# Retention, mixture of experts and rational network on one core: counts of groups of six in the natural blocks' banks, and a product bank for the conversions beside the first expert

## The chip, the cores and the metric

The kernel runs on one core of one Trainium2 chip. The metric is the device time of one launch in microseconds (us), median of several runs. Engines: PE (TensorE, matrix products), DVE (VectorE), ACT (ScalarE), POOL (GpSimd), SP (SyncE, which issues DMAs). Matrix products land in PSUM, eight banks of 512 four-byte words in each of 128 partitions; DVE and ACT empty them.

## What is computed

```python
for t in range(S):                                   # _attn_ref: 4 x 8 heads, 768 steps, 64 wide
    state = gamma * state + outer(k[t], v[t])
    y[t] = scale * q[t] @ state
# x = y as (3072, 512)
logits = x @ w_gate                                  # _moe_ref: 8 experts, 384 tokens each
for idx in np.argsort(-logits.flatten()):            # greedy: best logit first, while the expert has room
    ...
out[mask] = np.maximum(x[mask] @ w1[e], 0) @ w2[e]
h = out @ w_in                                       # _moe2_ref
g = P(h) / (Q(h) + 1e-6)                             # P cubic, Q quadratic in |h|
return g @ w_out
```

## The kernel before, in words

**Stage one** (0 to about 170 us) takes the 24 blocks of 128 tokens in turn (`for j in range(NCH)`). For a block PE does, in an order written out by hand: `trans` (two transposes, L352), `scores` (L382), `state` (L395), `natural` of the block before (L424: back to token-major, with the eight logits beside it) and `yout` (L407, L411). The transposes and the natural blocks share three PSUM banks, the pool `pt` (`NPT = 3`): `trans` takes two, `natural` two (one emptied by ACT, L428; one by DVE, L426). `scores`, `state`, `yout` and the conversions have banks of their own.

Beside this, two jobs run in stage one. *Conversions:* the weights `w_in` and `w_out` come as 64-bit numbers; `conv` (L239) makes float32 words of a 128x512 block with three DVE operations, L241, L243 and L244, and one on ACT, L242. Its intermediate words `t1` lie in a PSUM tile `cvp` in stage one. *Counts:* for the routing, `first(c0, c1)` (L448) makes one-hot choices and 128 threshold comparisons for a group of blocks (six DVE operations, L438 to L454), and `first_count` (L457) lets PE count them (L460) into a bank of its own from `pt`, and adds the result to `cn0` (L462). Groups are of three blocks, and the counts follow three blocks after.

**Stage two** starts with the routing of the first expert. Then the experts run one after another. For each, `mm1` (w1, L814) and `mm2` (w2) make the expert's output in eight steps; then sixteen steps of `mm3` (w_in, L814), `rat1` to `rat3` (the rational function: ACT L868 to L870, POOL L871, DVE L872, L873, L888 to L890), `gsplit`, and `mm4` (w_out, L910) three steps behind. `xt` (L798) transposes the next expert's tokens. `mm1`, `mm3` and `xt` share three PSUM banks, the tag `w` with `bufs=3`; the accumulators take four banks, the routing one. The bank of `mm3(i)` is free when L873 of step i has read it.

The routing of the next expert is a chain of small DVE operations and small PE products (L628, L641 and others), of which `chain.hop()` puts two links at a time into PE's order. PE waits at a link until DVE has done the link before.

Beside the first expert alone, twelve conversions are still to do: six blocks of `w_out` in the first eight steps (`job_conv`, tiles `xg`) and six of `w_in` in the sixteen (`in_conv_a`, tiles `w2r`). Here `conv` is called without `t1`, so that all its words lie in SBUF.

The orders of PE, ACT and POOL are those in which the code is written (`manual_schedule`; ACT's from stage two on). DVE's order is set by the scheduler, from its own estimates, with the chain given priority (`PRIO`).

Of the kernel before, what the change touches and what calls it, by code (L numbers as in the profile page):

```python
# [24 lines left out]
NCH = B * NC  # L25
# [27 lines left out]
CST = 2  # L53
CRAMP = 2
ET = mybir.EngineType
PROENG = {ET.PE, ET.Pool}
# [118 lines left out]
def moe_kernel(ctx, tc, q, k, v, w_gate, w1, w2, w_in, w_out, a, b, cf, ci, out):  # L175
# [74 lines left out]
    with ExitStack() as pst:  # L250
# [164 lines left out]

        def natural(j):

            if j < 0:
                return
            x = XN[j] = wk.tile([128, HP, 128 + E], F32, name="xn", bufs=3)  # L420
            for g in range(2):
                p = pp.tile([128, 2, 128 + E], F32, name="pt", bufs=NPT)
                for e in range(2):
                    nc.tensor.matmul(p[:, e, :], XT[j][:, 2 * g + e, :], IW[:, 2 * g + e, :], start=True, stop=True)  # L424
                if g:
                    nc.vector.tensor_copy(x[:, 2:4], p)  # L426
                else:
                    nc.scalar.activation(x[:, 0:2], p, AF.Copy)  # L428
            nc.vector.tensor_reduce(Sl[:, j, :], x[:, :, 128:].rearrange("p a e -> p e a"), axis=AX.X, op=OP.add)
            for r in range(2):  # L430
                nc.sync.dma_start(xd[j * 128:(j + 1) * 128, :].rearrange("(q r) (a f) -> r q a f", r=2, a=HP)[r],
                                  x[r * 64:r * 64 + 64, :, 0:128])
# [14 lines left out]

        CM0 = {}  # L448

        def first(c0, c1):  # L450
            onehot(c0, c1)
            w = c1 - c0
            cm = CM0[c0] = wk.tile([128, w, J0], BF16, name="cm")
            nc.vector.tensor_tensor(cm, m[:, c0:c1, None].to_broadcast([128, w, J0]),  # L454
                                    cit[:, 0:J0].bitcast(F32)[:, None, :].to_broadcast([128, w, J0]), op=OP.is_ge)

        def first_count(c0, c1):  # L457
            p = pp.tile([J0, E], F32, name="pt", bufs=NPT)
            for c in range(c0, c1):
                nc.tensor.matmul(p, CM0[c0][:, c - c0, :], oh[:, c, :], start=c == c0, stop=c == c1 - 1)  # L460
            if c0:
                nc.vector.tensor_tensor(cn0, p, cn0, op=OP.add)  # L462
            else:
                nc.vector.tensor_copy(cn0, p)

        load(0, "qk")
# [18 lines left out]
        for j in range(NCH):  # L485
# [12 lines left out]
            state(j)  # L498
            natural(j - 1)
            if j % 3 == 0 and j >= 3:  # L500
                first(j - 3, j)
                if j > 3:
                    first_count(j - 6, j - 3)
            if j == NCH - 1:
                first_count(NCH - 6, NCH - 3)
            yout(j)
# [3 lines left out]
        while db < da:  # L510
            conv_b(db)
            db += 1
        first(NCH - 3, NCH - 1)
        natural(NCH - 1)
        first_count(NCH - 3, NCH - 1)
        first(NCH - 1, NCH)
# [269 lines left out]
    def w2_split(n, f):  # L786
# [4 lines left out]
        w2_load(n, f + 2)  # L791

    def xt(n, t):
        if t == 0:
            XTS[n] = mp.tile([128, 2, KD, CAP], F32R, name="xT", bufs=1)
        p = ps.tile([128, KD, 128], F32, name="w", bufs=3)
        for d in range(KD):
# [20 lines left out]
    def mm1(n, f):  # L818
        p = ps.tile([128, CAP], F32, name="w", bufs=3)
        w, x = W1S[n, f], XTS[n]  # L820
# [30 lines left out]
    def mm3(n, i):  # L851
        p = US[n, i] = ps.tile([128, CAP], F32, name="w", bufs=3)
        y = YS[n]
# [92 lines left out]
    def job_conv(j):  # L946
        if j < NLATE:
            CA[j] = mp.tile([128, KD * 128], I32, name="xg", bufs=TB)
            conv(rawx[:, j % 3], CA[j], mp.tile([128, KD * 128], I32, name="xg", bufs=TB))
            job_load(j + 3)  # L950
# [15 lines left out]
    def in_conv_a(j):  # L966
        if j >= len(NORES):
            return
        CA[j] = mp.tile([128, KD * 128], I32, name="w2r")
        conv(RX[j], CA[j], mp.tile([128, KD * 128], I32, name="w2r"))  # L970
        in_load(j + 2)
# [139 lines left out]
```

## Time and profile before

| | |
|---|---|
| median of 3 runs | 1081.24 us (1080.59 to 1082.49) |
| the profiled execution's own time | 1081.6 us |
| its span, first to last instruction | 1079.7 us |
| PE busy, share of the span | 1010.1 us, 94% |
| DVE, ACT, POOL busy | 775.5, 698.5, 629.1 us |
| stage one ends (last `yout`) | about 169 us |
| first expert, first product to last | about 202 to 334 us |
| every later expert | about 106 us |

The span is 1.9 us shorter than that execution's time. Busy times overlap. A matmul's record is the time in which it is in the engine, so that neighbouring records overlap by some tens of ns.

### The profile page before, as it was taken

How to read it: one execution, taken by the hardware profiler on the slowest of the kernel's cores; microseconds unless marked ns; L12 is line 12 of the kernel's file. 1: busy time of each engine (PE TensorE's matmuls, PEld its weight loads, DVE VectorE, ACT ScalarE, POOL GpSimd, SP SyncE). 2: the span in 40 equal slices, each digit the busy share in tenths (PEclk: the TensorE clock that was granted, in tenths of full speed). 3: DMA queues.
4: the chain of work that ended last, by engine and by line, in shares of the span. 5: the costliest groups of instructions: out<-in, count | busy, mean ns of one | idle time of the engine just before them, and what ended most of it. 6: DMA issues, size and time to landing. Idle time of an engine off the chain costs nothing.

```text
span 1079.7 us, 18280 instructions
## 1 busy us (share of the span) xinstructions
PE 1010.1 (94%) x6278; PEld 922.2 (85%) x6278; DVE 775.5 (72%) x1862; ACT 698.5 (65%) x1365; POOL 629.1 (58%) x612
## 2 busy tenths in 40 slices
PE   6999885679889999999999999999999999999995
PEld 5888774678779989998999899999998999989984
DVE  4899887678994788478747874787578756751773
ACT  6889882346684488458745874587358736873883
POOL 5677662464686367635663666366736663666452
PEclk9999997699999999999999999999999999999998
DMA  9999862523333212321232124212422142223110
GB/s 191 244 250 252 226 162 89 151 93 96 100 127 118 88 50 79 117 88 59 69 121 86 59 69 127 79 59 70 137 69 68 60 137 70 88 65 110 50 59 29
DMA packets 142028, 115.01 MB, mean 107 GB/s; under 512 B 56560, under 2 KB 122352, under 8 KB 141936
## 3 DMA queue, kind: packets, MB, share of 16 engines
q1 hardware_dynamic: 131184, 76.10, 26.7%
q0 software_dynamic: 10752, 37.75, 10.5%
q8 instruction: 49, 0.80, 0.3%
q14 instruction: 43, 0.35, 0.1%
HBM read 98.10 MB, written 15.73 MB: 105 GB/s over the span
## 4 chain that ended last, share of the span: by engine, by line
PE 63%; DVE 7%; ACT 2%; issue 2%; POOL 1%; POOLq 0%; DVEq 0%
PE w L814 30%; PE acc L910 22%; PE acc L814 8%; PE pr L628 1%; PE w L798 1%; DVE hg L825 1%; DVE cm L592 1%; ACT hg L824 0%; DVE t L872 0%; DVE t L890 0%; POOL qq L871 0%; DVE yT L842 0%; DVE qq L888 0%; DVE acc L889 0%; DVE pr L583 0%
## 5 line engine op out<-in xcount | busy, mean ns | idle before, releaser
L910 PE MATMUL acc<-woh,hg 128*128 128x512 f32 x1152 | 290.2, 397 | 4.8 <-ACT hg L895 4.5
L910 PEld LDWEIGHTS acc<-woh,hg 128*128 128x128 f32 x1152 | 212.8, 188 | 49.7 <-ACT hg L895 7.0
L871 POOL TENSOR_TENSOR qq<-qq,z 128x384 f32<-128x384 f32 x127 | 129.4, 1019 | 165.2 <-ACT z L869 163.7
L814 PE MATMUL w<-yT,wih 128*128 128x384 f32 x960 | 179.6, 339 | 0.1
L896 POOL TENSOR_TENSOR hg<-t,hg 128x384 fp32r<-128x384 f32 x127 | 131.6, 1037 | 81.4 <-ACT hg L895 53.1
L814 PEld LDWEIGHTS w<-yT,wih 128*128 128x128 f32 x960 | 166.4, 188 | 3.8 <-DVE yT L842 0.7
L814 PE MATMUL w<-xT,w1s 128*128 128x384 f32 x768 | 149.7, 343 | 0.6 <-ACT xT L800 0.6
L814 PE MATMUL acc<-hg,w2s 128*128 128x384 f32 x768 | 146.2, 339 | 0.3 <-DVE hg L825 0.3
L814 PEld LDWEIGHTS w<-xT,w1s 128*128 128x128 f32 x768 | 135.4, 192 | 1.9 <-ACT xT L800 0.8
L814 PEld LDWEIGHTS acc<-hg,w2s 128*128 128x128 f32 x768 | 132.7, 188 | 1.1 <-DVE hg L825 0.6
L888 DVE SCALAR_TENSOR_TENSOR qq<-qq,acc 128x384 f32<-128x384 f32 x128 | 70.8, 553 | 60.4 <-ACT acc L883 33.3
L248 POOL TENSOR_TENSOR w1s<-w1r,w1s 128x512 fp32r<-128x512 f32 x64 | 83.2, 1300 | 49.2 <-ACT w1s L247 48.4
L814 PE MATMUL w<-yT,wis 128*128 128x384 f32 x576 | 110.0, 339 | 1.1 <-DVE t L873 1.1
L248 POOL TENSOR_TENSOR w2s<-w2r,w2s 128x512 fp32r<-128x512 f32 x64 | 83.2, 1301 | 43.7 <-ACT w2s L247 43.4
L895 ACT ACTIVATE hg<-t 128x384 fp32r<-128x384 f32 x128 | 67.1, 525 | 63.9 <-DVE t L890 63.7
L814 PEld LDWEIGHTS w<-yT,wis 128*128 128x128 f32 x576 | 100.3, 188 | 3.7 <-DVE t L873 1.3
L868 ACT ACTIVATE qq<-w,rb 128x384 f32<-128x384 f32 x128 | 73.3, 573 | 36.9 <-PE w L814 35.6
L824 ACT ACTIVATE hg<-w 128x384 fp32r<-128x384 f32 x64 | 31.4, 490 | 92.1 <-PE w L814 92.1
L870 ACT ACTIVATE t<-w,ab 128x384 f32<-128x384 f32 x128 | 86.1, 673 | 0.0
L872 DVE TENSOR_TENSOR t<-w,t 128x384 f32<-128x384 f32 x128 | 70.4, 550 | 21.1 <-ACT t L870 21.1
L247 ACT ACTIVATE w2s<-w2r 128x512 fp32r<-128x512 f32 x64 | 40.2, 629 | 68.1 <-issue 41.7
L825 DVE SCALAR_TENSOR_TENSOR hg<-w,hg 128x384 fp32r<-128x384 f32 x64 | 35.6, 556 | 66.3 <-ACT hg L824 66.0
(183 smaller groups left out, 1761.7 us busy)
## 6 DMA issues: line engine op xcount, KB each, us to landing
wis<-wid POOLq DMA_DIRECT2D x42, 512.0 KB, 3.5
w1r<-in_moe_w_dram SPq DMA_DIRECT2D x64, 256.0 KB, 2.8
w2r<-in_moe_w_dram SPq DMA_DIRECT2D x64, 256.0 KB, 2.7
qn<-in_q_dram SPq DMA_DIRECT2D x48, 128.0 KB, 4.1
kn<-in_k_dram SPq DMA_DIRECT2D x24, 256.0 KB, 4.6
vn<-in_v_dram SPq DMA_DIRECT2D x24, 256.0 KB, 5.0
xd<-xn SPq DMA_DIRECT2D x48, 128.0 KB, 3.9
raw<-in_moe_w_in_dram SPq DMA_DIRECT2D x10, 512.0 KB, 6.5
```

The lines of the kernel that those rows point to most:

```text
L247: nc.scalar.activation(dst[:, 0], src, AF.Copy)
L248: lo_eng.tensor_tensor(dst[:, 1], src, dst[:, 0].bitcast(F32), op=OP.subtract)
L814: nc.tensor.matmul(o, w[a], x[b], start=first and n[key] == 1, stop=last and n[key] == total)
L825: HLO[n, f] = nc.vector.scalar_tensor_tensor(h[:, 1], p, 0.0, h[:, 0].bitcast(F32), op0=OP.max, op1=OP.subtract).ins
L868: nc.scalar.activation(qq, p, AF.Square, scale=rb)
L870: nc.scalar.activation(t, p, AF.Identity, bias=ab[:, 2:3], scale=ab[:, 3:4])
L871: light(n, i).tensor_tensor(qq, qq, z, op=OP.add)
L872: nc.vector.tensor_tensor(t, p, t, op=OP.mult)
L888: nc.vector.scalar_tensor_tensor(qq, qq, QC, r, op0=OP.add, op1=OP.mult)
L895: nc.scalar.activation(g[:, 0], t, AF.Copy)
L896: light(n, i).tensor_tensor(g[:, 1], t, g[:, 0].bitcast(F32), op=OP.subtract)
L910: nc.tensor.matmul(ACC[t], g[:, x, t * 128:(t + 1) * 128], woh[:, i, y], start=i == 0 and x + y == 0, stop=i == NF2 - 1 and x == 1)
```

## The change

Four edits. First, groups in stage one end at the blocks of `CUTS` (six, six, six, three), then two and one as before. `cm`, the comparisons of a group, is twice as long and has one buffer in place of two. Second, the counts of the first four groups go into the last eight words of the bank that the natural block's second half holds, behind its 272 words; they stand behind that half's products in PE's order, in the first `natural` from two blocks after the group's end. Third, the conversions beside the first expert get a PSUM tile for `t1`, `ctile()`, tag `x`, one bank. Fourth, to make room the tag `w` has two banks: beside the first expert `mm1` and `mm3` use these two alone, the second expert's `xt` uses `x`, and after that `wtile` deals the banks out in turn, w, w, x.

```diff
+CUTS = (0, 6, 12, 18, 21)
...
-        def natural(j):
+        def natural(j, count=None):
...
-                p = pp.tile([128, 2, 128 + E], F32, name="pt", bufs=NPT)
+                pb = pp.tile([128, 512], F32, name="pt", bufs=NPT)
+                p = pb[:, 0:2 * (128 + E)].rearrange("p (a f) -> p a f", a=2)
                 for e in range(2):
                     nc.tensor.matmul(p[:, e, :], XT[j][:, 2 * g + e, :], IW[:, 2 * g + e, :], start=True, stop=True)
                 if g:
+                    if count:
+                        products(pb[0:J0, 512 - E:], *count)
                     nc.vector.tensor_copy(x[:, 2:4], p)
+                    if count:
+                        add_counts(pb[0:J0, 512 - E:], count[0])
...
-            cm = CM0[c0] = wk.tile([128, w, J0], BF16, name="cm")
+            cm = CM0[c0] = wk.tile([128, w, J0], BF16, name="cm", bufs=1)
...
-            natural(j - 1)
-            if j % 3 == 0 and j >= 3:
-                first(j - 3, j)
-                if j > 3:
-                    first_count(j - 6, j - 3)
-            if j == NCH - 1:
-                first_count(NCH - 6, NCH - 3)
+            natural(j - 1, GROUPS.pop(0) if GROUPS and j >= GROUPS[0][1] + 2 else None)
+            if j in CUTS[1:]:
+                c0 = CUTS[CUTS.index(j) - 1]
+                first(c0, j)
+                GROUPS.append((c0, j))
...
+    WN = [0]
+
+    def wtile(shape, first=False):
+        if not first:
+            WN[0] += 1
+        x = not first and WN[0] % 3 == 0
+        return ps.tile(shape, F32, name="x" if x else "w", bufs=1 if x else 2)
+
+    def ctile():
+        return ps.tile([128, 512], I32, name="x", bufs=1)
+
     def xt(n, t):
...
-        p = ps.tile([128, KD, 128], F32, name="w", bufs=3)
+        p = ps.tile([128, KD, 128], F32, name="x", bufs=1) if n == 1 else wtile([128, KD, 128])
...
     def mm1(n, f):
-        p = ps.tile([128, CAP], F32, name="w", bufs=3)
+        p = wtile([128, CAP], n == 0)
...
     def mm3(n, i):
-        p = US[n, i] = ps.tile([128, CAP], F32, name="w", bufs=3)
+        p = US[n, i] = wtile([128, CAP], n == 0)
...
-            conv(rawx[:, j % 3], CA[j], mp.tile([128, KD * 128], I32, name="xg", bufs=TB))
+            conv(rawx[:, j % 3], CA[j], mp.tile([128, KD * 128], I32, name="xg", bufs=TB), ctile())
...
-        conv(RX[j], CA[j], mp.tile([128, KD * 128], I32, name="w2r"))
+        conv(RX[j], CA[j], mp.tile([128, KD * 128], I32, name="w2r"), ctile())
```

**PE in stage one, around the counts.** Before, block 9: the counts (L460) of blocks 3 to 5 have a bank of their own, `pt_1113`, and stand ahead of `yout` (L407).

```order
L395 MATMUL ps_781<-vt_836,kn_656 64x64 x8
L424 MATMUL pt_1095<-IW_122,xt_1021 128x136 x2
L424 MATMUL pt_1099<-IW_122,xt_1021 128x136 x2
L460 LDWEIGHTS cm_809
L460 MATMUL pt_1113<-oh_98,cm_809 128x8
L407 MATMUL py_1118<-qt_972,Sb1_115 128x128 x4
```

In the change, block 8, the counts (L468) of blocks 0 to 5:

```order
L428 MATMUL pt_985<-IW_122,xt_911 128x136 x2
L428 MATMUL pt_989<-IW_122,xt_911 128x136 x2
L468 LDWEIGHTS cm_802
L468 MATMUL pt_989<-oh_98,cm_802 128x8
```

The two L460 rows stand three times in the program, the two L468 rows six times. The counts now write `pt_989`, the bank that the natural block's second half already holds, and take no fifth bank of the three.

**DVE beside the first expert's sixteen steps.** Before, the first conversion of `w_in` (L241, L243) and the chain's links around it:

```order
L635 TENSOR_TENSOR cmk<-pr,cft 64x128
L241 TENSOR_SCALAR w2r<-w2s 128x512
L636 TENSOR_REDUCE ce<-cmk 64x16
L243 SCALAR_TENSOR_TENSOR w2r<-w2s,w2r 128x512
L637 TENSOR_TENSOR ex<-ce,pr 64x128
```

In the change (L243 and L245 are the lines of the same two operations there):

```order
L648 TENSOR_TENSOR cmk<-pr,cft 64x128
L243 TENSOR_SCALAR x<-w2s 128x512
L649 TENSOR_REDUCE ce<-cmk 64x16
L245 SCALAR_TENSOR_TENSOR x<-w2s,x 128x512
L650 TENSOR_TENSOR ex<-ce,pr 64x128
```

The places are the same here; the conversion's words go to `x`, in PSUM. Further on, DVE's order differs by one to three places between links, conversions and the rational function.

## Rows read from the trace of the kernel before

**Rows 1.** The page, part 1: busy us, share of the span, instructions.
```profile
PE 1010.1 (94%) x6278; PEld 922.2 (85%) x6278; DVE 775.5 (72%) x1862; ACT 698.5 (65%) x1365; POOL 629.1 (58%) x612
```
**Rows 2.** Stretches: us, busy by engine, PE clock (1.00 full), DMA share, GB/s.
```profile
54.60:163.30 108.70, 97.55 (x1060) 87.38 (x1057) 97.41 (x183) 94.66 (x203) 73.47 (x62) 1.00 0.90 220
205.00:255.00 50.00, 42.43 (x236) 40.55 (x236) 37.07 (x88) 22.37 (x42) 26.89 (x19) 0.95 0.31 96
255.00:314.00 59.00, 51.89 (x261) 43.96 (x260) 56.69 (x126) 43.67 (x86) 41.71 (x39) 1.00 0.33 103
```
**Rows 3.** PE's counts, 54.6 to 163.3: count, busy us, mean ns, idle before, releasers.
```profile
L460 PE MATMUL pt<-oh,cm 128*128 128x8 bf16 x18 | 1.3, 166 | 9.0 <-ACT xn L428 8.5 <-DVE xn L426 0.5
```
**Rows 4.** PE's other wait of weight there: us in total, times, longest.
```profile
PE pt L352 <- DVE kh L371: 2.3, 4, 0.6
```
**Rows 5.** ACT's longest wait in the same stretch.
```profile
ACT xt L414 <- PE py L411: 8.4, 8, 2.3
```
**Rows 6.** DVE, same stretch, by form: count, busy us, mean ns, idle before.
```profile
L241 DVE TENSOR_SCALAR cvp<-raw 128x512 int32<-128x512 int32 x15 | 10.3, 686 | 0.0
L243 DVE SCALAR_TENSOR_TENSOR cvp<-raw,cvp 128x512 int32<-128x512 int32 x15 | 10.3, 685 | 0.0
L244 DVE CUSTOM_DVE_ANT_0 cv<-cvp,cv 128x1024 uint16<-128x1024 uint16 x15 | 10.2, 682 | 0.1
...
L440 DVE TENSOR_TENSOR t<-t,cft 128x24 f32<-128x24 f32 x6 | 5.3, 878 | 0.0
L439 DVE TENSOR_TENSOR t<-Sl,m 128x24 f32<-128x24 f32 x6 | 5.0, 826 | 0.2
L443 DVE TENSOR_TENSOR oh<-t,mraw 128x24 bf16<-128x24 f32 x6 | 3.4, 564 | 0.2
...
L462 DVE TENSOR_TENSOR cn<-pt,cn 128x8 f32<-128x8 f32 x5 | 0.8, 163 | 1.2 <-PE pt L460 1.2
```
**Rows 7.** DVE's conversions beside the first expert, by form, 205 to 345 us.
```profile
L243 DVE SCALAR_TENSOR_TENSOR xg<-yT,xg 128x512 int32<-128x512 int32 x6 | 6.7, 1120 | 0.0
...
L244 DVE CUSTOM_DVE_ANT_0 xg<-xg 128x1024 uint16<-128x1024 uint16 x6 | 6.0, 998 | 1.8 <-ACT xg L242 1.8
...
L243 DVE SCALAR_TENSOR_TENSOR w2r<-w2s,w2r 128x512 int32<-128x512 int32 x6 | 5.4, 896 | 0.0
L241 DVE TENSOR_SCALAR xg<-yT 128x512 int32<-128x512 int32 x6 | 5.3, 888 | 0.9 <-POOL woh L248 0.9
L244 DVE CUSTOM_DVE_ANT_0 w2r<-w2r 128x1024 uint16<-128x1024 uint16 x6 | 5.1, 858 | 0.0
...
L241 DVE TENSOR_SCALAR w2r<-w2s 128x512 int32<-128x512 int32 x6 | 3.2, 530 | 0.5 <-DMA w2s<-in_moe_w_in_dram 0.5
```
**Rows 8.** PE's waits, 205 to 255 us.
```profile
PE pr L641 <- DVE ex L637: 4.2, 3, 2.9
PE pr L628 <- DVE pr L598: 3.3, 2, 1.9
```
**Rows 9.** In order of time (start, us, instruction), and the stretch 230 to 240.
```profile
226.45 1.48 DVE L241 TENSOR_SCALAR xg<-yT 128x512 int32<-128x512 int32 x1 [0.45 <-POOL woh L248]
...
228.13 1.49 DVE L243 SCALAR_TENSOR_TENSOR xg<-yT,xg 128x512 int32<-128x512 int32 x1
...
230.04 3.43 PE L814 MATMUL w<-xT,w1s 128*128 128x384 f32 x12
...
230.00:240.00 10.00, 10.00 (x51) 9.90 (x52) 6.43 (x18) 3.21 (x6) 5.43 (x4) 0.83 0.10 28
```
**Rows 10.** In order of time: `mm3` of steps 7 and 13, and L873 of step 5.
```profile
275.51 2.27 PE L814 MATMUL w<-yT,wis 128*128 128x384 f32 x12
...
278.59 0.60 DVE L873 SCALAR_TENSOR_TENSOR t<-t,ab,w 128x384 f32<-128x384 f32 x1
...
307.61 2.38 PE L814 MATMUL w<-yT,wis 128*128 128x384 f32 x12 [1.05 <-DVE t L873]
```
**Rows 11.** One link of the chain, whole run: ns min/median/max, first and last start.
```profile
L583 DVE SCALAR_TENSOR_TENSOR pr<-ni,cit x7: 171/183/3025, 203.1 to 795.5; 128x16 int32<-128x16 int32 x7
```

More of the change, by code (lines that the diff above doesn't have):

```diff
@@ L448, in moe_kernel @@
         CM0 = {}
+        GROUPS = []
         def first(c0, c1):
@@ L452, in first, with products, add_counts @@
             w = c1 - c0
-            cm = CM0[c0] = wk.tile([128, w, J0], BF16, name="cm")
+            cm = CM0[c0] = wk.tile([128, w, J0], BF16, name="cm", bufs=1)
             nc.vector.tensor_tensor(cm, m[:, c0:c1, None].to_broadcast([128, w, J0]),
                                     cit[:, 0:J0].bitcast(F32)[:, None, :].to_broadcast([128, w, J0]), op=OP.is_ge)
-        def first_count(c0, c1):
-            p = pp.tile([J0, E], F32, name="pt", bufs=NPT)
+        def products(p, c0, c1):
             for c in range(c0, c1):
                 nc.tensor.matmul(p, CM0[c0][:, c - c0, :], oh[:, c, :], start=c == c0, stop=c == c1 - 1)
+        def add_counts(p, c0):
             if c0:
@@ L464, in first_count @@
                 nc.vector.tensor_copy(cn0, p)
+        def first_count(c0, c1):
+            p = pp.tile([J0, E], F32, name="pt", bufs=NPT)
+            products(p, c0, c1)
+            add_counts(p, c0)
         load(0, "qk")
@@ L512, in moe_kernel @@
             db += 1
-        first(NCH - 3, NCH - 1)
+        first(CUTS[-1], NCH - 1)
         natural(NCH - 1)
-        first_count(NCH - 3, NCH - 1)
+        first_count(CUTS[-1], NCH - 1)
         first(NCH - 1, NCH)
```

## The prediction

> **What bounds the kernel now.** I read the page first, then the busy time by stretch, then the waits of each engine in the stretches that the change touches, then single instructions in order of time. PE is busy for 94% of the span [rows 1], so only the rest can be won, and the question is where PE stands idle. The stretches answer it [rows 2]. In 54.6 to 163.3 us, blocks 7 to 22 of stage one, PE, DVE and ACT are busy for 97.55, 97.41 and 94.66 us of 108.70: three engines about equally full, each held up by the others now and then. In 205 to 255 us, the first expert's eight steps, PE lacks 7.6 of 50.0 us. In 255 to 314 us, most of its sixteen steps, DVE is busy for 56.69 of 59.00 us: here DVE is the bound, and PE lacks 7.1. In the later experts, which the change leaves as they are but for the banks' names, PE hardly waits; time that is won before them arrives at the end undiminished.
>
> In stage one nearly all of PE's idle time is of one kind. Before the counts it waits 9.0 us, mostly for ACT to empty a natural block's bank [rows 3], because the counts want a fifth bank in a block where three serve four. The only other wait of weight is 2.3 us for DVE's L371 [rows 4]. ACT, in turn, waits 8.4 us for `yout` [rows 5], which stands behind the counts on PE. So PE stands still for ACT, and then ACT for PE.
>
> **The counts' bank.** The change writes the counts where the natural block already lies, so nothing is waited for that the block did not need itself. PE's counts need the group's choices from DVE; these are two blocks old by then, some 14 us at 6.8 a block (108.70 for 16). PE can gain at most the 9.0 us. ACT sets a nearer limit: it is busy 94.66 us and idle 14.0, of which 8.4 is the wait for `yout`; with that gone and the other 5.6 us of idle left, the stretch is 100.3 us long, 8.4 shorter. Against it stands that DVE now empties the second half's bank only after six products of 166 ns [rows 3] and keeps it for the addition of 163 ns [rows 6], in all up to 1.2 us, and before, the bank went free without either. The neighbouring instructions overlap, and I take half, 0.6, three times in the stretch: 1.8. The term is **-6.6**. Its ends are 0 (ACT's lag remains the pace, and the wait only moves to the next bank) and -11.3 (9.0 and the 2.3 of rows 4).
>
> **The longer groups.** Three small operations of a group, L439, L440 and L443, take 13.7 us for six groups [rows 6], 2.3 each, whatever the group's length to first order (24 or 48 columns). The change has four groups in the loop where seven were: 7 us less work on DVE, two groups' worth of it in the stretch. The comparisons' total work stays, and three additions fall away. Behind ACT's limit above this buys nothing by itself; it is what could take the 2.3 us of rows 4, and it stands in the range only. The one buffer of `cm` is free again when the counts are done, four blocks before the next group of six needs it. For the group of blocks 21 and 22, the counts of 18 to 20 stand in block 23, one block ahead; for the last one, L454 waits for the counts before it, which PE does at once. I count both at nothing; the cover is the small operations behind them in DVE's order, and without it the last one costs about one product.
>
> **The conversions' words in PSUM.** Beside the first expert the three operations take 0.89, 1.12 and 1.00 us (the blocks of `w_out`) and 0.53, 0.90 and 0.86 (those of `w_in`); in stage one, with the words in PSUM and POOL about as busy (68% there, 54 and 71% here [rows 2]), each takes 0.68 to 0.69 [rows 6, 7]. So six conversions fall from 18.0 to 12.3 us and six from 13.7 to 12.3: **5.7 us less on DVE** in the eight steps, **1.4 less** in the sixteen.
>
> The same row shows a price as well: L241 on `w2r` takes 0.53 with its words in SBUF and takes 0.69 in PSUM. The Trainium skill (Perfetto Trace Analysis, Optimizing Scalar/DVE Operations) speaks against this edit: it gives DVE about 60 ns of overhead on SBUF and 125 on PSUM, by which, as an estimate, 36 operations would grow by 65 ns, 2.3 us in all. The trace agrees for that one form and contradicts it for the five others. The skill's SBUF — State Buffer, Who interferes with whom, has the reason: an operation of two SBUF inputs waits out a POOL instruction that reads SBUF, and one with a PSUM operand does not; by it the sum is the 7.1 us saved above.
>
> *In the eight steps* DVE is not full (37.07 of 50), and only what stands before a link of the chain counts. PE waits there five times for a link, 7.5 us [rows 8]. The longest, 2.9, ends when L637 is done, and ahead of that DVE did L241 in 1.48 and L243 in 1.49 us [rows 9]; at 0.69 each this link comes 1.6 earlier. L241 also waited 0.45 there for POOL to free its tile, which the words in PSUM do not need. For the other waits I take a third of their 4.6 us, 1.5, the share by which the three operations shrink (5.7 of 18.0). Together 3.5. After the longest wait PE's clock is at its lower level (1.2 of 2.4 GHz) for a part of the stretch, 0.83 on average in 230 to 240, and one `mm1` takes 3.43 us [rows 9], against 2.3 for its like at full clock [rows 10]. Half of that 1.1, if the shorter gap keeps the clock, makes 0.5; but the DVE order shifts a conversion's third operation ahead of a link at two places, 0.7 each at most, and I take 0.5 back. The term is **-3.5**; its ends are 0 (PE was about to wait for something else) and -7.5 (all of rows 8).
>
> *In the sixteen steps* DVE is the bound, so that its 1.4 us count in full. One link there took 3.02 us, where the median of the seven like it is 0.18 [rows 11]; it is a matter of what POOL does at that moment, and half of the 2.8 is taken: 1.4.
>
> **Two banks for `mm3`.** With three, `mm3(i)` needs the reading of step i-3; with two, that of i-2. The trace of before shows what this meets: `mm3` of step 7 starts at 275.5, and L873 of step 5 ends at 279.2 [rows 10]. So PE would have to start 3.7 us later there; ten steps show such a lateness, this being the largest. By itself this costs nothing: DVE is the bound and has the reading of the step between still to do when `mm3` starts, and at step 13 PE is down to waiting for L873 with three banks too, 1.05 us [rows 10], so that both versions leave this stretch at the same reading. What it can cost is a link of the chain that stands behind the late `mm3` on PE and is in turn waited for on DVE. I take half of 3.7, once: 1.8. The ends are 0 and the price under the third rival. The sixteen steps together: -1.4 -1.4 +1.8 = **-1.0**.
>
> The sum is -6.6 -3.5 -1.0 = -11.1. The profiled execution took 1081.6, which gives 1070.5; the median of before is 0.4 below that execution, so I predict **1070.1**.
>
> **Rivals.**
> 1. *ACT paces stage one anyway.* At 94.66 of a possible 100 us ACT has little air; removing the counts' wait lets PE run into a wait for the next bank that ACT empties. For it: eight waits of ACT, but six counts; against it: ACT idles only because of PE's standstill. Stage one then gives 2, the rest as forecast: 1081.2 - 2 - 4.5 = 1074.7.
> 2. *The conversions were covered.* The banks' exchange gives nothing, since the links behind the conversions wait for PE's products as well. For it: DVE has 13 us of idle time in the eight steps. Only stage one's term stays: 1074.6. That the words do not come out faster in PSUM belongs here too; stage one's rows speak against it.
> 3. *The two banks bind: slower.* Each late `mm3` makes a link late, DVE stands still for it, and L873, on which the next `mm3` depends, comes later still. Ten steps at half of 3.7 are 18.5 us: 1081.2 - 12.9 + 18.5 = 1086.8. It decides from 1.3 us of DVE idle time per step on. Beside it, a rule of the Trainium skill (Perfetto Trace Analysis, Matmuls) has independent products rotate through banks so that emptying one overlaps the next, which taking a bank away goes against. Against this rival: DVE's own work for a step lies between one reading and the next, so that it has other work while PE is late.
>
> **How the numbers follow.** The forecast has 0.60, the rivals 0.15, 0.14 and 0.11. Measurements of this kernel tell about 0.2%, 2.2 us, from no change. The forecast and the first two rivals are faster; of the third I put 0.07 slower and 0.04 so partial that it just balances. So faster 0.89, same 0.04, slower 0.07. The range: the gain is largest if all of rows 3 and 4 and most of rows 8 go, -18.8, of which I do not expect more than -17, 1064; its other side takes in both partial rivals and a little of the third, 1077. Some 0.8 lies in between.
>
> **What would show it.** Right: L460's successor has no wait for ACT, ACT's wait for `yout` is below 2 us, and blocks 7 to 22 take some 102 us. The twelve conversions show 0.68 to 0.69 three times each. Waits for links in the eight steps are near 4 us. In the sixteen steps `mm3` waits for L873 several times, by 1 to 4 us, while DVE stays as busy as it was. Wrong: a wait of PE for ACT's L428 before L352 as large as the one that went; DVE idle for PE's links for over 5 us in the sixteen steps; or a first expert as long as before in spite of shorter conversions.

## The result, and the profile after

The changed kernel takes **1068.46 us** (median of 4 runs, 1067.54 to 1069.34); the kernel before took 1080.91 beside it (4 runs, 1080.52 to 1082.49). The ratio is 0.9876, interval 0.9862 to 0.9890: 12.5 us less, where the prediction had 11.1 and a time of 1070.1. The profiled execution took 1068.97, its span 1066.0; the 3.0 us outside its span (1.9 before) are why spans differ by more than times.

The page, part 1, of the changed kernel [as rows 1]:

```profile
PE 1008.1 (95%) x6278; PEld 922.1 (87%) x6278; DVE 758.7 (71%) x1841; ACT 697.3 (65%) x1365; POOL 622.7 (58%) x612
```

PE does the same work in a span that is 13.7 us shorter. Where the time went is read from four marks in order of time: the start of the last `yout`, of the first expert's first `mm1`, of its first `mm3`, and of the second expert's first product into an accumulator.

| us | last `yout` | routing, to `mm1` | eight steps | sixteen steps | the rest |
|---|---|---|---|---|---|
| before | 167.96 | 34.01 | 46.80 | 85.17 | 745.7 |
| after | 162.88 | 34.13 | 41.83 | 81.25 | 745.9 |
| difference | -5.1 | +0.1 | -5.0 | -3.9 | +0.2 |
| forecast | -6.6 | 0 | -3.5 | -1.0 | 0 |

So every place that the prediction named gave something and no other did, but the three sizes are not those forecast. The 6.6 were forecast for blocks 7 to 22 alone: there it is 3.9 (108.70 to 104.77), 1.6 came earlier (54.59 to 53.03) and 0.4 were lost behind. Part of the 1.6 is the start of stage one, which differs by 1.4 us between kernels with one and the same stage one. In the lines of the changed kernel L413 is `yout` (L411 before), L386 the masks (L384), L436 and L432 the natural block's two readings (L428, L426), L468 the counts (L460), L243, L245 and L246 the conversion on DVE (L241, L243, L244), L840 and L936 the products (L814, L910), L824 the transposes of `xt` (L798), L899 the reading of `mm3`'s bank (L873), L596 the link (L583).

The stretches that answer to [rows 2]: blocks 7 to 22 of stage one, most of the eight steps, and most of the sixteen (to `mm3` of step 14):

```profile
53.03:157.80 104.77, 98.19 (x1061) 88.66 (x1060) 91.03 (x168) 94.40 (x203) 75.14 (x62) 0.98 0.98 235
200.00:245.00 45.00, 40.80 (x232) 38.44 (x231) 31.86 (x88) 22.33 (x42) 24.02 (x19) 0.97 0.33 106
245.00:300.40 55.40, 51.63 (x265) 45.30 (x266) 53.08 (x126) 44.61 (x88) 37.44 (x38) 1.00 0.34 105
```

In the third, DVE has 3.61 us less to do in the same 126 instructions, and the stretch is 3.60 shorter than before; DVE is idle for 2.3 us of it in both. In the first, ACT has as much to do as before, DVE 6.4 us less, and the stretch is 3.9 shorter. PE's counts there, all of PE's waits [rows 3, 4], and ACT's for `yout` [rows 5], the waits with their total, number and longest:

```profile
L468 PE MATMUL pt<-oh,cm 128*128 128x8 bf16 x18 | 0.9, 167 | 0.0
```

```profile
PE py L413 <- DVE am L386: 3.3, 4, 1.8
PE pt L354 <- ACT xn L436: 1.3, 3, 0.7
PE pt L354 <- DVE kh L373: 1.1, 2, 0.6
PE pt L354 <- POOL QB L369: 0.9, 1, 0.9
```

```profile
ACT xt L416 <- PE py L413: 1.5, 3, 0.9
```

The 9.0 us before the counts are gone and ACT's 8.4 are 1.5. But PE now waits 3.3 us for DVE's masks, where it did not wait before, and 1.3 for the next bank that ACT empties. All its waits were 11.6 us [rows 3, 4, and 0.3 for L428] and are 6.6. The stretch gained less than these 5.0, and PE is busy for longer with the same work (98.19, before 97.55), because the granted clock fell to 0.50 in it for a while; the rows of this stand with the experiments.

The conversions beside the first expert [rows 7]:

```profile
L246 DVE CUSTOM_DVE_ANT_0 xg<-x,xg 128x1024 uint16<-128x1024 uint16 x6 | 4.1, 690 | 4.7 <-ACT xg L244 4.7
L245 DVE SCALAR_TENSOR_TENSOR x<-yT,x 128x512 int32<-128x512 int32 x6 | 4.1, 690 | 0.0
L245 DVE SCALAR_TENSOR_TENSOR x<-w2s,x 128x512 int32<-128x512 int32 x6 | 4.1, 687 | 0.1
L243 DVE TENSOR_SCALAR x<-w2s 128x512 int32<-128x512 int32 x6 | 4.1, 684 | 0.2 <-DMA w2s<-in_moe_w_in_dram 0.2
L243 DVE TENSOR_SCALAR x<-yT 128x512 int32<-128x512 int32 x6 | 4.1, 684 | 0.0
L246 DVE CUSTOM_DVE_ANT_0 w2r<-x,w2r 128x1024 uint16<-128x1024 uint16 x6 | 4.1, 683 | 0.1
```

All six forms take 0.68 to 0.69. PE's waits from 200 to 245 us [rows 8], then two stretches of 10 us in the middle of the eight steps, first of after, then those of before, counted from the first `mm1`:

```profile
PE pr L641 <- DVE pr L611: 2.1, 2, 1.0
PE pr L654 <- DVE ex L650: 1.8, 2, 1.0
```

```profile
217.00:227.00 10.00, 9.28 (x56) 8.68 (x55) 7.70 (x22) 5.46 (x11) 7.62 (x6) 1.00 0.42 133
227.00:237.00 10.00, 8.96 (x54) 8.46 (x53) 6.88 (x22) 4.47 (x9) 6.37 (x5) 1.00 0.00 0
```

```profile
222.00:232.00 10.00, 7.13 (x41) 6.77 (x40) 8.45 (x18) 4.44 (x8) 7.42 (x6) 0.94 0.42 133
232.00:242.00 10.00, 8.59 (x46) 8.18 (x45) 6.57 (x18) 4.61 (x9) 5.36 (x4) 0.89 0.00 0
```

The waits fell from 7.5 to 3.9 us, the longest from 2.9 to 1.0, and behind them the granted clock no longer leaves 1.00 (2.4 GHz).

In the sixteen steps PE now waits for `mm3`'s bank, five times:

```profile
PE w L840 <- DVE t L899: 4.0, 5, 1.5
```

and yet the stretch is shorter. PE's waits of `mm4` for ACT, here as they were before, are gone in exchange:

```profile
PE acc L910 <- ACT hg L895: 3.6, 5, 1.5
```

And behind the link (L583, L596) less is lost. `mm3` of steps 13 and 14 on PE: first of before, where `xt` between them waits, then of after, then of a kernel with three banks and a link of 0.17 us, in which L843 is `mm3` (link in PSUM, three banks, below).

```profile
313.73 0.66 PE L798 MATMUL w<-cft,xg 128*128 128x128 f32 x4 [1.65 <-DVE xT L801]
314.25 2.35 PE L814 MATMUL w<-yT,wih 128*128 128x384 f32 x12
```

```profile
295.76 2.36 PE L840 MATMUL w<-yT,wis 128*128 128x384 f32 x12
...
300.41 2.34 PE L840 MATMUL w<-yT,wih 128*128 128x384 f32 x12
```

```profile
304.25 2.37 PE L843 MATMUL w<-yT,wis 128*128 128x384 f32 x12 [1.01 <-DVE t L902]
...
308.92 2.33 PE L843 MATMUL w<-yT,wih 128*128 128x384 f32 x12
```

From `mm3` of step 13 to that of step 14 it is 6.6 us before (307.61 [rows 10] to 314.25), 4.65 after, and 4.67 with three banks and the short link. So these 2 us are the link's and not the banks': `xt` waited for a DVE that was held up for 3.02 us.

### The profile page after: what moved, and what is told of

Read it like the earlier page. It is cut to its first block, busy times and chain, and to the rows that moved or that the text cites. A ratio compares the mean times of both kernels' runs of the same rounds, so it can differ in the third digit from the quotient of the medians.

```text
span 1066.0 us, 18253 instructions
## 1 busy us (share of the span) xinstructions
PE 1008.1 (95%) x6278; PEld 922.1 (87%) x6278; DVE 758.7 (71%) x1841; ACT 697.3 (65%) x1365; POOL 622.7 (58%) x612
## 4 chain that ended last, share of the span: by engine, by line
PE 72%; DVE 10%; ACT 4%; issue 2%; DMA 1%; POOL 1%; POOLq 0%; DVEq 0%; ACTq 0%
PE w L840 24%; PE acc L936 24%; PE x L840 10%; PE acc L840 8%; PE pr L641 1%; DVE cm L605 1%; DVE hg L851 1%; ACT hg L850 1%; PE pa L384 1%; PE pt L354 1%; PE pr L619 0%; PE w L824 0%; PE x L824 0%; DVE t L898 0%; DVE t L916 0%
## 5 line engine op out<-in xcount | busy, mean ns | idle before, releaser
L936 PE MATMUL acc<-woh,hg 128*128 128x512 f32 x1152 | 289.3, 396 | 0.8 <-ACT hg L921 0.8
L936 PEld LDWEIGHTS acc<-woh,hg 128*128 128x128 f32 x1152 | 213.4, 188 | 43.5 <-ACT hg L921 1.8
L840 PE MATMUL acc<-hg,w2s 128*128 128x384 f32 x768 | 145.9, 339 | 0.3 <-DVE hg L851 0.3
L840 PEld LDWEIGHTS acc<-hg,w2s 128*128 128x128 f32 x768 | 132.4, 188 | 1.1 <-DVE hg L851 0.6
L840 PE MATMUL w<-yT,wih 128*128 128x384 f32 x624 | 117.9, 339 | 0.9 <-DVE t L899 0.8
L840 PE MATMUL w<-xT,w1s 128*128 128x384 f32 x600 | 116.6, 343 | 0.6 <-ACT xT L826 0.6
L840 PEld LDWEIGHTS w<-yT,wih 128*128 128x128 f32 x624 | 108.1, 188 | 3.6 <-DVE t L899 1.8
L250 POOL TENSOR_TENSOR w1s<-w1r,w1s 128x512 fp32r<-128x512 f32 x64 | 82.6, 1291 | 46.8 <-ACT w1s L249 46.0
L840 PEld LDWEIGHTS w<-xT,w1s 128*128 128x128 f32 x600 | 105.9, 192 | 1.9 <-ACT xT L826 0.8
L908 ACT ACTIVATE z<-qq,qcb 128x384 f32<-128x384 f32 x128 | 77.7, 607 | 7.9 <-POOL qq L897 7.3
L840 PE MATMUL w<-yT,wis 128*128 128x384 f32 x408 | 78.1, 339 | 3.2 <-DVE t L899 3.2
L916 DVE SCALAR_TENSOR_TENSOR t<-t,ab,acc 128x384 f32<-128x384 f32 x128 | 78.4, 613 | 3.4
L840 PEld LDWEIGHTS w<-yT,wis 128*128 128x128 f32 x408 | 70.9, 188 | 5.8 <-DVE t L899 4.2
L915 DVE SCALAR_TENSOR_TENSOR acc<-qq,acc 128x384 f32<-128x384 f32 x128 | 71.6, 560 | 3.3
L909 ACT ACTIVATE acc<-z 128x384 f32<-128x384 f32 x128 | 63.5, 496 | 4.1
```

The source lines that it names most:

```text
L250: lo_eng.tensor_tensor(dst[:, 1], src, dst[:, 0].bitcast(F32), op=OP.subtract)
L840: nc.tensor.matmul(o, w[a], x[b], start=first and n[key] == 1, stop=last and n[key] == total)
L908: nc.scalar.activation(z, qq, AF.Ln, bias=qcb)
L909: nc.scalar.activation(r[:, :CAP], z, AF.Exp, scale=-1.0)
L915: nc.vector.scalar_tensor_tensor(r, qq, 2.0, r, op0=OP.subtract, op1=OP.mult, reverse0=True)
L916: nc.vector.scalar_tensor_tensor(t, t, ab[:, 0:1], r, op0=OP.add, op1=OP.mult)
```

## The experiments

Twelve kernels, each in five rounds beside the kernel before, in three groups; that kernel's median was 1082.36, 1082.05 and 1082.22 there, so the ratios are what to compare. The changed kernel's was 0.9876. The marks of the table above, read in each profile:

| kernel | median us | ratio, interval | last `yout` | eight | sixteen | link us |
|---|---|---|---|---|---|---|
| first two edits alone | 1078.30 | 0.9956, .9939 to .9973 | 161.55 | 47.92 | 85.00 | 3.02 |
| last two edits alone | 1073.20 | 0.9911, .9894 to .9928 | 167.76 | 41.62 | 81.41 | 1.04 |
| two banks, words in SBUF | 1073.94 | 0.9923, .9909 to .9938 | 161.24 | 46.79 | 82.48 | 0.83 |
| threes in banks | 1069.17 | 0.9875, .9856 to .9893 | 163.50 | 41.37 | 81.21 | 1.04 |
| `xt` in the two banks | 1073.03 | 0.9917, .9900 to .9933 | 163.04 | 41.84 | 87.81 | 1.01 |
| sixes, own bank | 1072.91 | 0.9919, .9907 to .9931 | 168.48 | 41.23 | 81.28 | 1.04 |
| late comparisons | 1067.87 | 0.9867, .9850 to .9883 | 162.67 | 41.56 | 81.29 | 1.04 |
| late comparisons, threes | 1068.05 | 0.9872, .9856 to .9887 | 163.52 | 41.87 | 81.32 | 1.03 |
| link in PSUM, three banks | 1074.67 | 0.9930, .9918 to .9943 | 163.13 | 48.02 | 82.92 | 0.17 |
| link in PSUM | 1069.12 | 0.9876, .9859 to .9893 | 163.70 | 41.75 | 81.22 | 0.17 |
| pieces of two | 1070.20 | 0.9894, .9879 to .9909 | 164.93 | 41.73 | 81.40 | 1.04 |
| both last | 1071.07 | 0.9898, .9885 to .9912 | 165.01 | 41.60 | 81.34 | 0.17 |

The later stretches of the changed kernel repeat to some 0.3 us, stage one does not: with one and the same stage one, the changed kernel and six of these end it at 161.2 to 163.7. A part of that is its start, the rest the clock. In all seven PE waits for the masks in the same place, in the changed kernel here:

```profile
61.15 0.66 PE L413 MATMUL py<-am,vt 128*64 128x128 f32 x8 [1.77 <-DVE am L386]
```

Behind this wait the granted clock stands at 0.50 (1.2 of 2.4 GHz) for a while in five of the profiled executions, and stays at 1.00 in two. The changed kernel, and the first two edits alone:

```profile
63.00:65.00 2.00, 2.00 (x13) 1.58 (x9) 1.90 (x5) 1.59 (x4) 1.30 (x2) 0.50 1.02 297
```

```profile
62.00:64.00 2.00, 1.45 (x15) 1.04 (x14) 1.94 (x4) 1.56 (x4) 0.80 (x1) 1.00 1.02 296
```

From `yout` of block 6 to that of block 22 the two without the fall take 103.9 us, the five with it 104.6 to 105.0, so that the fall costs some 0.9. Threes in banks take 105.2 without a fall, the kernel before 108.7 without one; sixes with their own bank take 109.8 with one. What decides whether the clock falls is not shown: the waits ahead of it are the same.

**The first two edits alone.** The diff of the change without its third and fourth edit.

> Only the first two edits (groups of six, counts in the natural block's bank); three banks for mm1, mm3 and xt, and the conversions' words beside the first expert in SBUF, as before. Theory A, the two halves of the change act apart from each other: the last yout starts at 162.9 as in the changed kernel, from there on the times of before return, and the median is 5 us below that of before, 1075 to 1077. Rival B, the time won in stage one is lost again at the first expert because the transfers or POOL are not ready earlier: within 2 us of before, 1079 to 1081. Rival C, most of the changed kernel's gain comes from here: 1071 or less.

Theory A by the marks: 0.44% less, 4.8 us, stage one ends 1.3 us earlier still than in the changed kernel, the sixteen steps take what they took. The median of 1078.30 lies between the ranges of A and B; the kernel before was at 1082.36 beside it. The eight steps are 1.1 us longer than before: the granted clock falls to 0.50 twice in them (at 211.2 and 224.9), in the kernel before once (at 230.9).

**The last two edits alone.** The diff without its first and second.

> Only the last two edits (the conversions' words in a bank of PSUM beside the first expert, two banks for mm1 and mm3 there); stage one as before, with groups of three and the counts' own bank. Theory A: the last yout starts at 168.0 as before, the stretch from the first mm1 to the first mm3 is 41.8 us (46.8 before), the sixteen steps 81.2 (85.2 before), and the median is 7 to 9 us below that of before, 1072 to 1074. Rival B, the first expert gained only since stage one ended earlier: 1078 or more.

Theory A, a little beyond its figure: 0.89% or 9.6 us. The parts add up: 0.9956 times 0.9911 is 0.9867, within the interval of the whole.

**Two banks, words in SBUF.** The changed kernel without `ctile`:

```diff
-            conv(rawx[:, j % 3], CA[j], mp.tile([128, KD * 128], I32, name="xg", bufs=TB), ctile())
+            conv(rawx[:, j % 3], CA[j], mp.tile([128, KD * 128], I32, name="xg", bufs=TB))
...
-        conv(RX[j], CA[j], mp.tile([128, KD * 128], I32, name="w2r"), ctile())
+        conv(RX[j], CA[j], mp.tile([128, KD * 128], I32, name="w2r"))
```

> The changed kernel with the conversions' words beside the first expert in SBUF again; the two banks for mm1 and mm3 stay, and no conversion uses the third bank. Against the changed kernel's 1068.5. Theory A, the words in PSUM make the gain and the two banks cost next to nothing: the eight steps take 46 to 47 us again, the sixteen 84 to 86, so 8 to 10 us more, 1076 to 1078, the same as the first two edits alone. Rival B, the two banks cost 4 us or more that the words pay back: 1080 to 1084. Rival C, the gain beside the first expert is one of the instructions' order and not of the words' place: 1068 to 1071.

None of the three in full. The eight steps are theory A: 46.79, as before, with the same waits as before for the same links:

```profile
PE pr L641 <- DVE pr L611: 3.3, 2, 1.9
PE pr L654 <- DVE ex L650: 3.2, 2, 2.9
```

So there the words' place is all of it. The sixteen steps are not: 82.48, 2.5 us less than with three banks, without a single word in PSUM. Two things could have made them faster, `xt`'s own bank or the link, which takes 0.83 us here in place of 3.02; two of the later kernels ask which.

**Threes in banks.** `CUTS = (0, 3, 6, 9, 12, 15, 18, 21)` in the changed kernel.

> The changed kernel with groups of three blocks again (CUTS = 0, 3, 6, ... 21), the counts still in the natural block's bank. Theory A, the bank alone makes the gain of stage one, and DVE has room for three more groups' small operations: PE waits less for the masks (L386) behind a group, and the median is between 1067 and 1070. Rival B, the longer groups are needed, because DVE, at 91 of 105 us in blocks 7 to 22, has no room for some 7 us more: stage one 3 to 5 us longer, 1071.5 to 1074.

Theory A by the time: no difference to groups of six that can be told (0.9875 against 0.9876). In part this is the clock, which fell behind the masks in the changed kernel's profiled execution and not in this one; without a fall, sixes take 103.9 us for blocks 7 to 22 and threes 105.2. And A's reason is not borne out: the wait for the masks stays at 3.0 us in three waits. On DVE, L447, L448 and L451 on 24 columns take 12.5 us for seven groups (3.2, 5.1, 4.2), where the four groups of the changed kernel take 8.9.

**`xt` in the two banks.** In the changed kernel,

```diff
-        p = ps.tile([128, KD, 128], F32, name="x", bufs=1) if n == 1 else wtile([128, KD, 128])
+        p = wtile([128, KD, 128], n == 1)
```

> The changed kernel, except that the transposes of the second expert's tokens (xt, beside the first expert's sixteen steps) go to the two banks of mm1 and mm3; the third bank has the conversions alone. So far three kernels with two banks for mm3 show sixteen steps of 81.2 to 82.5 us, whether the words lie in PSUM or in SBUF, and two kernels with three banks 85.0 and 85.2. Theory A, the gain of some 2.5 us comes from xt having a bank of its own, so that mm3 no longer stands behind it in one ring of banks: here the sixteen steps take 84 us or more, the median is 3 us or more above the changed kernel's, 1071.5 or more. Rival B, it comes from the order of DVE, in which the one link (L596) meets a gap of POOL and takes 0.8 to 1.0 us in place of 3.0: it depends on where that link lies here; with about 1 us the sixteen steps take 81 to 82 and the median is 1068 to 1070, with 3 us some 83.5 and 1071.

Theory A by its numbers: the link stays short (1.01), and the sixteen steps take 87.81, 6.6 us more than with `xt`'s own bank; by the ratios it is 0.41%, 4.4 us. The place, steps 12 to 14 on PE in order of time:

```profile
291.35 2.25 PE L840 MATMUL w<-yT,wih 128*128 128x384 f32 x12
295.60 0.60 PE L824 MATMUL w<-cft,xg 128*128 128x128 f32 x4
299.35 4.21 PE L840 MATMUL w<-yT,wis 128*128 128x384 f32 x12 [3.15 <-DVE t L899]
306.24 0.60 PE L824 MATMUL w<-cft,xg 128*128 128x128 f32 x4
```

`mm3` of step 13 has to wait 3.15 us for the reading of step 12, since the transposes hold the other bank; behind the wait it takes 4.21 us in place of 2.36. The two stretches around its start give the reason (PE busy, then the granted clock):

```profile
295.00:299.00 4.00, 1.21 (x9) 0.84 (x7) 3.54 (x10) 4.00 (x9) 3.69 (x5) 0.91 0.48 149
299.00:304.00 5.00, 4.65 (x14) 4.55 (x15) 3.12 (x8) 1.22 (x3) 3.12 (x3) 0.50 0.38 108
```

PE was busy for 1.21 of 4 us, and the clock then stands at 0.50, 1.2 of 2.4 GHz, for all of the next 5: in this execution a wait of 3 us cost twice that. The run gives the price of `xt` in a ring of two. It does not show what the theory said, that `xt`'s own bank gains against a ring of three: no kernel here has three banks for `mm3` and one more for `xt`.

**Sixes, own bank.** The counts of the changed kernel's groups, in the same place of PE's order, get a bank of the three again:

```diff
-            natural(j - 1, GROUPS.pop(0) if GROUPS and j >= GROUPS[0][1] + 2 else None)
+            natural(j - 1)
+            if GROUPS and j >= GROUPS[0][1] + 2:
+                first_count(*GROUPS.pop(0))
```

> The changed kernel, but the counts have a bank of their own again out of the three, in the same place of PE's order, behind the natural block; groups of six stay. Theory A, the bank makes stage one's gain: PE waits for ACT's L436 or so before each of the three counts in blocks 7 to 22, by 1 to 2 us, and the last yout starts 2 to 4 us later than in the changed kernel (162.9), the median is 1070.5 to 1073. Rival B, the fewer and longer groups make the gain, and the bank nothing: within 1 us of the changed kernel, 1067.5 to 1069.5.

Theory A: by the ratios 0.43%, 4.6 us, above the changed kernel, and stage one ends at 168.48, no earlier than before and 5.6 later than in the changed kernel, where theory A had 2 to 4. PE's waits there:

```profile
PE pt L468 <- ACT xn L436: 4.4, 3, 1.7
PE py L413 <- DVE am L386: 3.2, 4, 1.7
PE pt L354 <- ACT xn L436: 2.3, 4, 0.9
```

Without the bank, groups half as many give nothing: 109.8 us for blocks 7 to 22, some 108.9 without the clock's fall in it, against 108.7 before.

**Late comparisons**, with groups of six and of three: L463 moved into a function of its own, called one block later.

```diff
+            if GROUPS and j == GROUPS[-1][1] + 1:
+                compare(*GROUPS[-1])
```

> The changed kernel with the comparisons of a group (L463, 1.2 to 1.8 us on DVE) one block later than its one-hot choices, still a block before the counts. Theory A, behind a group of six PE waits for the scores' masks (L386, 3.3 us in four waits) because DVE does the group's 5 us in one piece, and with two pieces that wait is half as large or less: stage one 1.5 to 3 us shorter, 1065.5 to 1067.5. Rival B, PE is held up by the sum of DVE's work and not by its pieces: within 1 us of the changed kernel, 1067.5 to 1069.5.

> The same with groups of three blocks. With the comparisons beside the choices, groups of three gave 1069.2, as groups of six did. Theory A (pieces matter): each piece of DVE is some 1.5 us, no wait for L386 above 0.5, the median 1065 to 1067.5. Rival B (the sum matters): 1068 to 1070, as with groups of three before.

Neither theory was tried: DVE's order here is the scheduler's, and the traces show the comparisons right behind L447, in the block in which they stood before. Both runs are repeats of their parents, and show how far the ratio of one order moves between groups of runs: 0.9876 and 0.9867, 0.9875 and 0.9872.

**The link's table in PSUM**, with the first two edits alone (three banks), and in the changed kernel:

```diff
+    o1 = CI_OFF["b", 1][0]
+    ptab = prb[:, 296:296 + 2 ** CI_OFF["b", 1][1]].bitcast(I32)
+    nc.vector.tensor_scalar(ptab, cit[:, o1:o1 + 2 ** CI_OFF["b", 1][1]], 0, None, op0=OP.bitwise_or)
...
-                    nc.vector.scalar_tensor_tensor(pre, ni.to_broadcast([128, J]), 0x7FFFFFFF, tab,
+                    nc.vector.scalar_tensor_tensor(pre, ni.to_broadcast([128, J]), 0x7FFFFFFF, ptab if n else tab,
```

> The first two edits alone (three banks, words in SBUF, sixteen steps of 85.0 us), and the table that the first link after a threshold's start reads (L596, 3.02 us there) is copied once into free columns of the routing's bank, so that the link has one input in SBUF in place of two. In every theory L596 falls to 0.2 us here if it is POOL that holds it up. Theory A, most of what the sixteen steps gained by the banks (4.5 us in steps 12 to 16) comes from xt's own bank and not from this link: the sixteen steps stay between 84 and 85, the median within 1.5 us of 1078.3. Theory B, the link's stall is the larger part of it: the sixteen steps fall to 82.5 or less, the median to 1076 or less.

> The changed kernel with the same table in the routing's bank. L596 takes 1.03 us there; it should take 0.2. As DVE is the bound of the sixteen steps, they become 0.5 to 0.8 us shorter (81.25 now), and the median 1067.5 to 1068.2 by that; if the stall was covered, no difference.

With three banks the sixteen steps fall from 85.00 to 82.92: 2.1 of the link's 2.85 us were on the path. By the steps that lies between the theories, by the median (1074.67) it is theory B. Two banks with the words in SBUF and a link of 0.83 us take 82.48, so that beside the link the two banks and `xt`'s own give only 0.4, and PE's waits over the sixteen steps are 6.3 us in both. In the changed kernel the same edit gives nothing (81.22 against 81.25): its 1.03 us are covered.

**Pieces of two**, and **both last** (with the link's table): choices and comparisons of two blocks at a time, as soon as their logits are there, so that DVE cannot do them in one piece; the counts in groups of six as in the change.

```diff
+            for g0, g1 in zip(CUTS, CUTS[1:]):
+                if g0 < j <= g1 and ((j - g0) % 2 == 0 or j == g1):
+                    piece(g0, g1, j - 2 + (j - g0) % 2, j)
```

> The changed kernel, counts in groups of six as there, but the choices and comparisons of a group are made on DVE two blocks at a time, as soon as their logits are there (the run that wrote the comparisons one block later left DVE's order as it was, so that it tried nothing). Each piece is some 1.7 us in place of 5. Theory A, PE's waits for the masks (L386, 3.3 us in four) come from the piece of 5 us: they fall below 1.5 us in all, the last yout starts 1.5 to 3 us earlier (162.9), the median 1065.5 to 1067.5. Rival B, PE is held up by the sum of DVE's work, which grows by some 4 us: 1068 to 1070.

> The two last edits together, in search of a faster version: if both give what theory A and the link's length say, 1065 to 1067; if neither does, 1068 to 1069.

Rival B, and slower than it said: the medians are 1070.20 and 1071.07, where it had 1068 to 1070 and 1068 to 1069. The waits for the masks are shorter each, but six, and as long in all; DVE's three small operations take 19.7 us for eleven pieces (8.9 for the four groups in the change):

```profile
PE py L413 <- DVE am L386: 3.1, 6, 0.8
```

```profile
L448 DVE TENSOR_TENSOR t<-t,cft 128x16 f32<-128x16 f32 x11 | 8.0, 726 | 0.0
L451 DVE TENSOR_TENSOR oh<-t,mraw 128x16 bf16<-128x16 f32 x11 | 7.0, 633 | 0.4
L447 DVE TENSOR_TENSOR t<-Sl,m 128x16 f32<-128x16 f32 x11 | 4.7, 424 | 0.3
```

Stage one ends at 164.9 and 165.0, later than in any of the seven with groups of six in one piece. No version was found that beats the changed kernel.

## Why the prediction was right, point by point

The sign and the sum were right, the time lies 1.6 us below the forecast and well inside the range. That the sum is so near is in part luck: of the three terms one was too large and two too small (-5.1, -5.0 and -3.9 by the marks, for -6.6, -3.5 and -1.0), and the errors cancel in part.

**The counts' bank: -6.6 forecast, -3.9 in the stretch that it was forecast for, -5.1 over all of stage one.** The mechanism is shown: with the bank and groups of three the gain is there, with groups of six and no bank it is not. The step that failed is the limit. I took ACT as next (100.3 us, less a give-back of 1.8), and counted DVE's groups at nothing behind it. ACT's work is unchanged at 94.4, but the stretch is 104.8: PE waits 3.3 us for DVE's masks, in every version with the counts in these banks (3.0 to 3.3), and behind them the clock can fall, some 0.9 us in the changed kernel's profiled execution. Of the give-back of 1.8, which stood for DVE emptying the second half later, nothing is seen: no wait of PE names L432. It was too large to begin with, since six products of 166 ns do not take 1.0 us: their records overlap by far more than tens of ns, and rows 3 have 1.3 us for 18 of them. The 1.3 us of wait for ACT's L436 are the first rival's, in small; by it only 2 us would have been won, and it is out.

**The longer groups: nothing forecast, 0.2 to 1.2 us measured.** Without the bank they give none. With it blocks 7 to 22 take 105.2 us with threes, and 103.9 with sixes, or 104.6 to 105.0 where the clock falls; the medians tell no difference. That the three operations cost about the same per group held (2.3 forecast, 8.9 for four here). What I left out is that more of them do cost: with eleven pieces in place of four the stretch takes 106.8.

**The words in PSUM, eight steps: -3.5 forecast, -5.0 measured.** All of it is the words': ten kernels with them take 41.2 to 41.9, four without 46.8 to 48.0, with two banks or three (46.8 with one fall of the clock in them, 47.9 and 48.0 with two). The durations came as read from stage one (0.68 to 0.69), and the Trainium skill's rule of more overhead on PSUM (Perfetto Trace Analysis, Optimizing Scalar/DVE Operations) holds here for one form of six: L241 on `w2r`, 0.53 before, 0.68 now; the five others fell. For L241 on `xg` (0.89 to 0.68) the reason given in the prediction does not serve, since this operation has one SBUF input and not two; its reason is open. The terms that were mis-sized are the two that I halved or gave back. The clock: I took half of 1.1 for `mm1`'s 3.43 us, and the granted clock now stays at 1.00, so that all of it came. And the 0.5 that I gave back for DVE's order did not show: the waits inside the eight steps fell from 6.5 to 2.8, 3.7 by themselves. The second rival, covered conversions, is out.

**The sixteen steps: -1.0 forecast, -3.9 measured.** The mechanism held in the main: DVE has 3.61 us less to do in the stretch, and the stretch is 3.60 shorter. Of its operations in the sixteen steps, the conversions take 12.3 us in place of 13.7, the 1.4 that were forecast. The link takes 1.03 in place of 3.02: I had taken half of 2.8, and 2.0 came; alone, with three banks, it was worth 2.1. The term that failed is the cost of two banks. I charged 1.8 for a link behind a late `mm3`. `mm3` now waits for 4.0 us, but PE's waits as a whole fell from 8.1 to 5.0 over the sixteen steps, and DVE stands idle no longer than before. That "both versions leave this stretch at the same reading" was near the truth: `mm3` of step 13 starts 58.6 us after the first with three banks and a link of 0.17, 58.2 after it with two banks, the words in SBUF and a link of 0.83, and the sixteen steps take 82.92 and 82.48. So no run shows a price of two banks where `xt` has its own. DVE is not the bound to the end, though: from step 12 on PE waits for nothing in the changed kernel, and 0.86 us less on DVE (link in PSUM) won nothing there. The marks on PE mislead here. From the first `mm3` to that of step 12 PE takes 51.5 us with three banks and the short link and 53.6 with two banks and the words in SBUF, from there to the end 31.4 and 28.9. With three banks PE runs ahead and then waits for DVE at step 13 (1.0 us), so that this alone does not show a gain by `xt`'s own bank; whether there is one was not separated. With two banks for `mm3` it is needed: `xt` in the ring of two costs 6.6 us, the third rival's mechanism, at a place that I had not named. The last 1.2 us come with the words (82.48 to 81.25); their own operations are only 0.2 us shorter than in that kernel, which leaves DVE's other order there, and this was not separated.

**What would show it.** Right: no wait before the counts; ACT's wait for `yout` 1.5; the conversions; the waits for links, 3.9 where I had said near 4; and five waits of `mm3` with DVE at 53.1 of 55.4 us, as busy as before, though they are of 0.4 to 1.5 us and not of 1 to 4. Wrong: blocks 7 to 22 take 104.8 and not 102.

## What to carry to other kernels

A product that needs a bank of its own for a few words can go behind the data of a bank that is due anyway; the wait for the bank goes, but ask which engine is fullest behind it, since it takes over part of the wait. When banks are dealt out anew, ask which engine is the bound: a product that starts later costs nothing while another engine has enough to do, as `mm3` here with two banks of its own, and a lot where it has not, as with `xt` in the same two. And a short DVE operation on a chain, with both operands in SBUF, is worth a look for its longest case and not its median.

## What the runs showed of the hardware

A DVE operation on 16 columns took 3.02 us, or 0.17, by the place of one operand. In the kernel before, in order of time, DVE and below it POOL:

```profile
307.47 3.02 DVE L583 SCALAR_TENSOR_TENSOR pr<-ni,cit 128x16 int32<-128x16 int32 x1
...
307.22 1.01 POOL L896 TENSOR_TENSOR hg<-t,hg 128x384 fp32r<-128x384 f32 x1
308.19 1.01 POOL L871 TENSOR_TENSOR qq<-qq,z 128x384 f32<-128x384 f32 x1
309.17 1.28 POOL L248 TENSOR_TENSOR wis<-w2r,wis 128x512 fp32r<-128x512 f32 x1
```

It begins inside the first of three POOL instructions that follow each other without a gap, and ends at 310.49, when the third has ended (310.45). With the table in PSUM, the same three instructions in the same order:

```profile
304.12 0.17 DVE L599 SCALAR_TENSOR_TENSOR pr<-ni,pr 128x16 int32<-128x16 int32 x1
...
303.87 1.02 POOL L925 TENSOR_TENSOR hg<-t,hg 128x384 fp32r<-128x384 f32 x1
304.84 1.02 POOL L900 TENSOR_TENSOR qq<-qq,z 128x384 f32<-128x384 f32 x1
305.82 1.29 POOL L250 TENSOR_TENSOR wis<-w2r,wis 128x512 fp32r<-128x512 f32 x1
```

In the changed kernel one POOL instruction (297.26 to 298.56) stands beside the link, and the link ends with it (298.59), after 1.03 us. The Trainium skill (SBUF — State Buffer, Who interferes with whom) says that a DVE instruction with two SBUF inputs contends with a GpSimd instruction that reads SBUF. The trace agrees, and shows that the wait lasts until POOL's row of instructions has a gap, three of them here.
